# Two six-head tiles for the last twelve heads of a memory attention, with a regrouping of phi(q) through DRAM, and a two-part memset ahead of the first products

## The chip, the cores and the metric

One core of a Trainium2 chip runs the kernel. The metric is the device time of one execution in microseconds; the time before is the median of three runs. All views of the profile come from one further execution, whose own time and span stand in the table below.

## The reference, cut to what matters

Two attention layers run side by side over 2048 positions, 640 channels, 32 heads of 20 channels, in bf16. Layer A works in four segments of 512 positions and carries a memory from segment to segment; layer B is a causal attention with a window of 256.

```python
for s in range(4):                       # layer A, per head
    p = softmax(qs @ ks.T * scale + mask)          # inside the segment
    a_dot = p @ vs
    pq = phi(qs)                                   # t + 1 if t > 0 else exp(t)
    a_mem = (pq @ M) / (pq @ z + 1e-6)             # what earlier segments left
    o = g * a_mem + (1 - g) * a_dot
    M = M + phi(ks).T @ vs                         # 20 x 20 per head
    z = z + phi(ks).sum(0)
out_A = o @ wo ;  out_B = windowed_softmax_attention(x_B) @ wo_B
```

The change touches only `pq @ M`, `pq @ z` and the updates of `M` and `z`.

## The kernel before, in words

**Stages.** Work goes in eight chunks of 512 positions, A0 B0 A1 B1 A2 B2 A3 B3. While one chunk is scored, the projections of the next run between its products. Scores of a head group (four heads, on rows 0, 32, 64 and 96) go from TensorE into a ring of three PSUM tiles `sc` (line 631); ScalarE takes the exponential into a ring of 12 SBUF tiles `pt` (line 647); GpSimd cuts the mask's triangles out of `pt` (`affine_select`, line 682), VectorE does so for small ends (line 664); TensorE multiplies `pt` with `v` (line 696, in the last chunk line 717); VectorE transposes the result (line 748); reciprocal and normalisation follow on VectorE and GpSimd (lines 768 to 802). Output goes through a DRAM scratch, a transposing DMA (line 835) and the last projection.

**Heads on tiles.** 128 rows hold four heads with a stride of 32 rows, so 20 of every 32 rows are used by heads 0 to 19 in five such tiles (`KT` = 5, groups `g` = 0 to 4). The 12 spare rows of every 32 hold the channels of the last 12 heads (`NM` = 20, `GAP` = 48). For the softmax part these rows are regrouped through DRAM into tiles 5 to 7 of `qA`, `kA`, `qB`, `kB` (`regroup`, lines 400 and 408: four stores and four loads each). For the memory part they are not: the list `MEM` names twelve pairs (row tile `m`, group `g`). Groups 0 to 4 have one pair each; group 5 has two, group 6 three, group 7 two.

**Memory.** `phi_q` (line 482) puts phi(q) into `pq`, five tiles of 128x512, by lines 463, 467 and 471. `phi_k` stores phi(k) to DRAM and loads it back transposed as `pkT` (line 497). `dm_job` (line 511) runs at the start of the B chunk that follows an A chunk, for segments 0, 1 and 2. It forms phi(k)^T v for all twelve pairs in two PSUM banks of six (line 526, 84 columns for a pair, 168 where two pairs share `m`), adds each bank to `mz` on VectorE (line 536), and has GpSimd write the masked bf16 copy `blk` (in the trace `MZ`): line 542 for the sums `z`, line 545 for `M`. `mem(g)` (line 725) then multiplies the pairs of a group with `pq`, in one bank: 12 products of 128x512 for a segment, in segments 1, 2 and 3.

**Order.** The order of instructions is not left to a scheduler. `Flow` holds a model of each engine's time (`on_pe`, `on_dve`, `on_pool`, `on_dma`), and `body` emits the next piece of work whose modelled time has come. Engines run their own queues in that order, so an instruction that waits holds back everything behind it on its engine. `yield t` in a job means that nothing more of the job is emitted before model time `t`; `mark` and `known` carry such times. DMAs are issued by SyncE, one queue in order, aside from a few on ScalarE's.

**Start.** `consts_mz` clears `blk` on VectorE (line 322), then `mz`. `warm_up` (line 215) multiplies these zeros while the first input is under way. `consts_mem` (line 273) makes the head masks `bm` on GpSimd, `consts_e` (line 303) the table `ez`.

Of the kernel before, what the change touches and what calls it, by code (L numbers as in the profile page):

```python
# [13 lines left out]
P = 128  # L14
# [13 lines left out]
QPOOL = 750.0  # L28
GAP = 48
NM = 20  # L30
MEM = [(0, 0), (1, 1), (2, 2), (3, 3), (4, 4), (0, 5),
       (1, 5), (1, 6), (2, 6), (3, 6), (3, 7), (4, 7)]
NE = 5
NOT = 4
NSC = 3
# [14 lines left out]
def mm_ns(n):  # L50
    return max(27.0, n / 2.4 + 2.5)
# [133 lines left out]
class _K:  # L185
# [29 lines left out]
    def warm_up(self, z):  # L215

        f = self.f
        ps, bi = self.bank()
        f.pe = max(f.pe, 1900.0)
        while f.pe + 700.0 < max(self.done[(0, "x", 0)], self.done[("wk_A", 0)]):  # L220
            self.wide(ps, z[:, 0:P], z[:, 0:L], L, True, True)
            f.flush()
        self.close(bi, f.seen)
# [49 lines left out]
    def consts_mem(self):  # L273

        nc, cp = self.nc, self.cp
        sel = cp.tile([P, self.KT, 12], F32, name="sel")
        own = cp.tile([P, 4], F32, name="own")

        def select(t, pattern, base, mul):
            nc.gpsimd.affine_select(out=t, in_=t, pattern=pattern, compare_op=ALU.is_ge,
                                    fill=0.0, base=base, channel_multiplier=mul)
        nc.gpsimd.memset(own[:], 1.0)
        select(own[:], [[-HD, 4]], 0, 1)
        select(own[:], [[HD, 4]], DH - 1, -1)
        nc.gpsimd.memset(sel[:], 1.0)
        for j in range(4):

            t, base = sel[HD * j:HD * j + HD], 12 * j - DH  # L290
            select(t, [[0, self.KT], [0, 12]], -DH, 1)
            select(t, [[GAP, self.KT], [-DH, 12]], base, 1)
            select(t, [[-GAP, self.KT], [DH, 12]], DH - 1 - base, -1)
        self.bm = bm = cp.tile([P, len(MEM), 4], F32, name="bm")
        self.ez = cp.tile([P, len(MEM), 4], F32, name="ez")
        nc.gpsimd.tensor_copy(out=bm[:, 0:self.KT, :],
                              in_=own[:].unsqueeze(1).to_broadcast([P, self.KT, 4]))
        flat = bm[:].rearrange("p x j -> p (x j)")
        for m, x, h0, n in ((0, 5, 0, 4), (1, 6, 0, 8), (2, 8, 4, 4), (3, 9, 4, 8), (4, 11, 8, 4)):
            nc.gpsimd.tensor_copy(out=flat[:, 4 * x:4 * x + n], in_=sel[:, m, h0:h0 + n])  # L300
        self.eps = cp.tile([P, G], F32, name="eps")

    def consts_e(self):

        nc, e = self.nc, self.e32
        for x0, x1, g in ((0, self.KT, 0), (5, 7, 5), (7, 10, 6), (10, 12, 7)):
            n = x1 - x0
            h = e[:, 4 * g:4 * g + (4 * n if x0 == 0 else 4)]
            h = (h.rearrange("p (x j) -> p x j", j=4) if x0 == 0 else
                 h.unsqueeze(1).to_broadcast([P, n, 4]))  # L310
            nc.gpsimd.tensor_tensor(out=self.ez[:, x0:x1, :], in0=self.bm[:, x0:x1, :], in1=h,
                                    op=ALU.mult)
        for j in range(4):
            rows = slice(HD * j, HD * j + HD)
            nc.gpsimd.tensor_single_scalar(
                out=self.eps[rows, :], in_=e[rows, :].rearrange(
                    "p (g j) -> p g j", j=4)[:, :, j], scalar=EPS, op=ALU.mult)

    def consts_mz(self):
        nc, cp = self.nc, self.cp  # L320
        self.blk = self.big.tile([P, len(MEM), 4, HD], BF16, name="MZ4")
        nc.vector.memset(self.blk[:], 0.0)
        self.mz = cp.tile([P, len(MEM), 4, VS], F32, name="mz")
        nc.vector.memset(self.mz[:], 0.0)

    def consts_ends(self):
# [184 lines left out]
    def dm_job(self, seg, pkT, v):  # L511


        nc, f = self.nc, self.f
        yield self.known("pkT", seg)
        W = 4 * VS
        half = len(MEM) // 2
        for x0 in (0, half):
            yield "bank"
            dM, bi = self.bank()  # L520
            x = x0
            while x < x0 + half:
                m, g = MEM[x]
                k = 2 if x + 1 < x0 + half and MEM[x + 1] == (m, g + 1) else 1
                for kt in range(LT):
                    nc.tensor.matmul(dM[:, W * (x - x0):W * (x - x0 + k)],
                                     lhsT=pkT[:, kt, P * m:P * m + P],
                                     rhs=v[:, kt, W * g:W * (g + k)],
                                     start=(kt == 0), stop=(kt == LT - 1))
                f.on_pe("full", 4 * mm_ns(max(W * k, P)), 4 * W * k)  # L530
                x += k
                if x < x0 + half:
                    yield 0.0
            dv = dM[:, 0:half * W].rearrange("p (x j c) -> p x j c", x=half, j=4)
            mz = self.mz[:, x0:x0 + half]
            nc.vector.tensor_tensor(out=mz, in0=dv, in1=mz, op=ALU.add)
            self.close(bi, f.on_dve(620.0, f.seen))
            f.open = False
        t = f.dve + 138.0
        yield self.known(2 * seg, "avs")  # L540
        blk, mz = self.blk, self.mz
        nc.gpsimd.tensor_tensor(out=blk[:, :, :, DH], in0=mz[:, :, :, DH], in1=self.ez[:],
                                op=ALU.mult)
        f.on_pool(150.0, t)
        nc.gpsimd.tensor_tensor(out=blk[:, :, :, 0:DH], in0=mz[:, :, :, 0:DH],
                                in1=self.bm[:].unsqueeze(3)
                                .to_broadcast([P, len(MEM), 4, DH]), op=ALU.mult)
# [468 lines left out]
    def body(self, xA, A_wq, A_wk, A_wv, A_wo, A_beta, xB, B_wqkv, B_wo, out2d):  # L1016
# [59 lines left out]
        for nm, rows in (("pk", D), ("qA", 12 * DH), ("kA", 12 * DH), ("qB", 12 * DH),  # L1076
                         ("kB", 12 * DH)):
# [38 lines left out]
        while True:  # L1116
# [34 lines left out]
            if pend:  # L1151
                n, g, what = pend[0]
                kind, c = chunks[n]
                if what == "tile":
                    ps_ = [p for x in range(4) for p in parts[(n, g[1] + x)]
                           if p[1] // P == g[0]]
                    need = [whole(p[6] for p in ps_), self.done.get((n, "v", g[1]))]
                elif what == "av":
                    ps_ = parts[(n, g)]
                    need = [whole(p[6] for p in ps_), self.done.get((n, "v", g))]  # L1160
                else:
                    need = [self.done.get(("dm", c - 1))] + [self.done.get((n, "pq", m))
                                                            for m, g_ in MEM if g_ == g]
# [198 lines left out]
```

## Time and profile before

| | |
|---|---|
| median of 3 runs | 353.37 us (351.37, 353.37, 354.8) |
| the profiled execution | 352.71 us, span 350.6 us |
| first score in each chunk | A0 9.29, B0 55.48, A1 95.31, B1 132.68, A2 176.71, B2 213.39, A3 254.99, B3 291.74 us |
| GpSimd busy without idle time | 128.8 to 170.2 us |
| last exponentials on ScalarE | up to 332 us |

Columns of a group's line: the line and engine, the operation, output and inputs, shapes, how often; then busy time in us and the mean of one in ns; then the idle time of that engine just before, and who ended it. PE is TensorE's products, PEld its weight loads, DVE VectorE, ACT ScalarE, POOL GpSimd, SP SyncE, whose DMA issues count as waiting but not as busy.

Four groups that the change touches:

```profile
L735 PE MATMUL m<-pq,MZ 128*128 128x512 bf16 x36 | 11.9, 384 | 1.4 <-DVE vB L573 0.6 <-DVE tt L748 0.4 <-DVE kB L445 0.3
L526 PE MATMUL m<-vA,pkT 128*128 128x84 bf16 x96 | 5.5, 201 | 0.0
L536 DVE TENSOR_TENSOR mz<-m,mz 128x504 f32<-128x504 f32 x6 | 4.0, 662 | 1.0 <-PE m L526 1.0
L542 POOL TENSOR_TENSOR MZ<-mz,ez 128x48 bf16<-128x48 f32 x3 | 2.1, 695 | 1.2 <-DVE mz L536 1.2
```

Products overlap: 384 ns is from the start of one to the end of its results, while the next one in a row starts 0.22 us later.

### The profile page before, as it was taken

What the parts mean: (1) busy time and instruction counts of PE and PEld (TensorE: products, weight loads), DVE (VectorE), ACT (ScalarE), POOL (GpSimd) and SP (SyncE); (2) the same over time, 40 slices, a digit from 0 to 9 for tenths busy, and PEclk for the clock granted to TensorE, in tenths of its full rate; (3) what the DMA queues carried; (4) which work ended last, traced back from release to release, by engine and by line L of the source; (5) the groups of instructions that cost most, each with busy time, mean ns of one, the idle gap of its engine ahead of it and who ended that gap; (6) DMA issues with size and microseconds to landing.
All of it is one profiled execution on the core that took longest, in us unless ns stands there. A gap on an engine that the chain in (4) does not pass through costs nothing.

```text
span 350.6 us, 13578 instructions
## 1 busy us (share of the span) xinstructions
PE 326.4 (93%) x5617; PEld 167.0 (48%) x5617; DVE 278.2 (79%) x557; ACT 315.0 (90%) x358; POOL 294.3 (84%) x592
## 2 busy tenths in 40 slices
PE   7999999989999999999999999988999999899994
PEld 2443435444544345455644436454543445566672
DVE  5687677999958999999967998997867999766621
ACT  2897499999999999999999999999999999989831
POOL 6589388988898989999898989899988989987720
PEclk9999999999999999999999999999999999999999
DMA  7945617526675133033794025030483032675773
GB/s 233 376 159 129 165 32 227 128 64 178 200 124 123 22 77 122 2 93 69 175 193 104 0 63 155 3 79 8 82 143 77 2 75 61 146 140 150 146 183 115
DMA packets 69374, 40.54 MB, mean 116 GB/s; under 512 B 48448, under 2 KB 67520, under 8 KB 69312
## 3 DMA queue, kind: packets, MB, share of 16 engines
q1 hardware_dynamic: 67584, 38.35, 45.2%
q10 hardware_dynamic: 1728, 1.32, 1.2%
q8 instruction: 44, 0.72, 0.9%
q14 instruction: 18, 0.15, 0.1%
HBM read 16.06 MB, written 16.38 MB: 93 GB/s over the span
## 4 chain that ended last, share of the span: by engine, by line
PE 48%; DVE 22%; POOL 11%; issue 6%; ACT 5%; DMA 5%; SPq 2%; DVEq 0%; ACTq 0%; POOLq 0%
PE m L735 30%; PE sc L631 9%; POOL pt L682 7%; PE m L696 6%; ACT pt L647 5%; DVE tt L748 4%; DVE pt L664 3%; DMA xT<-in_B_x_dram 2%; PE m L717 2%; DMA scr_o<-o 2%; POOL o L782 2%; DVE kB L445 1%; PE sc L735 1%; DVE pq L471 1%; DVE qA L445 1%
## 5 line engine op out<-in xcount | busy, mean ns | idle before, releaser
L647 ACT ACTIVATE pt<-sc 128x1024 bf16<-128x1024 f32 (+1 forms) x320 | 296.6, 1070 | 14.9 <-PE sc L631 12.9
L682 POOL TENSOR_SCALAR_AFFINE_SELECT pt<-pt 128x256 bf16<-128x256 bf16 x448 | 209.6, 495 | 36.0 <-ACT pt L647 30.8
L748 DVE STREAM_TRANSPOSE tt<-m 128x512 f32<-128x512 f32 x88 | 60.7, 706 | 19.4 <-PE m L696 9.4
L782 POOL TENSOR_TENSOR o<-tt,rr 128x320 bf16<-128x320 f32 x64 | 51.2, 801 | 2.8 <-DVE rr L774 2.7
L631 PE MATMUL sc<-qB,kB 20*64 20x64 bf16 (+2 forms) x1728 | 39.0, 217 | 1.2 <-issue 0.6
L735 PEld LDWEIGHTS <-xT 128*128 128x128 bf16 x320 | 28.7, 97 | 22.4 <-issue 11.6
L735 PEld LDWEIGHTS <-oT 128*128 128x128 bf16 x320 | 28.8, 97 | 17.2 <-issue 3.5
L631 PE MATMUL sc<-qA,kA 20*128 20x128 bf16 (+3 forms) x512 | 36.1, 300 | 0.9 <-ACT pt L647 0.3
L631 PEld LDWEIGHTS <-kB 20*64 20x64 bf16 (+1 forms) x1728 | 21.7, 98 | 25.1 <-issue 23.1
L735 PE MATMUL m<-wv_A,xT 128*128 128x320 bf16 x160 | 27.4, 300 | 3.7 <-DVE kA L445 2.0
L891 DVE CAST ot<-m 128x320 bf16<-128x320 f32 x46 | 21.9, 480 | 8.5 <-PE m L735 8.3
L735 PE MATMUL m<-xT,wq_A 128*128 128x512 bf16 x100 | 26.6, 386 | 1.1 <-DVE qA L445 0.9
L664 DVE TENSOR_TENSOR pt<-pt,ends 128x1024 bf16<-128x1024 bf16 x32 | 27.6, 875 | 0.0
L735 PE MATMUL m<-xT,wk_A 128*128 128x512 bf16 x100 | 27.2, 392 | 0.3
L735 PE MATMUL m<-xT,wBq 128*128 128x512 bf16 x100 | 25.8, 380 | 1.2 <-DVE tt L748 1.2
L735 PE MATMUL m<-xT,wBk 128*128 128x512 bf16 x100 | 25.3, 381 | 0.6 <-DVE kB L445 0.6
L735 PE MATMUL m<-wBv,xT 128*128 128x320 bf16 x160 | 25.6, 300 | 0.3 <-DVE tt L748 0.2
L631 PEld LDWEIGHTS <-kA 20*128 20x128 bf16 x512 | 10.5, 91 | 30.5 <-issue 29.8
L696 PE MATMUL m<-pt,vA 128*32 128x128 bf16 (+3 forms) x512 | 24.0, 302 | 0.5 <-POOL pt L682 0.3
L735 PE MATMUL m<-wo_A,oT 128*128 128x320 bf16 x120 | 20.8, 300 | 0.2 <-DVE ot L891 0.2
L802 POOL TENSOR_TENSOR o<-o,u 128x320 bf16<-128x320 bf16 x24 | 20.5, 854 | 0.0
L445 DVE CAST qB<-m 128x512 bf16<-128x512 f32 x20 | 13.6, 682 | 7.4 <-PE m L735 7.4
(87 smaller groups left out, 427.7 us busy)
## 6 DMA issues: line engine op xcount, KB each, us to landing
scr_o<-o SPq DMA_DIRECT2D x28, 160.0 KB
out_dram<-ot SPq DMA_DIRECT2D x27, 160.0 KB
xT<-in_B_x_dram SPq DMA_DIRECT2D x4, 720.0 KB
scr_pk<-e SPq DMA_DIRECT2D x15, 128.0 KB
xT<-in_A_x_dram SPq DMA_DIRECT2D x3, 640.0 KB
scr_kA<-kA SPq DMA_DIRECT2D x16, 60.0 KB
scr_qA<-qA SPq DMA_DIRECT2D x16, 60.0 KB
kA<-scr_kA SPq DMA_DIRECT2D x16, 60.0 KB
```

The lines of the kernel that those rows point to most:

```text
L445: nc.vector.tensor_copy(out=dst[:, m, at:at + L], in_=ps[:, :])
L631: nc.tensor.matmul(ps[j // 2][h0:h1, j % 2, c0:c0 + nq], lhsT=k[rows, g, kc + h0:kc + h1], rhs=q[rows, g, q0:q0 + nq], start=True, stop=Tr ...
L647: nc.scalar.activation(out=pt[:, :, lo:hi], in_=ps[i][:, :, lo:hi], func=ACT.Exp, scale=self.scale)
L664: nc.vector.tensor_tensor(out=blk, in0=blk, in1=self.ends[:].unsqueeze(1).to_broadcast([P, 1024 // SH, SH]), op=ALU.mult)
L682: nc.gpsimd.affine_select(out=blk, in_=blk, pattern=pat, compare_op=ALU.is_ge, fill=self.zero, base=base, channel_multiplier=mul)
L696: nc.tensor.matmul(O[HD * j:HD * j + HD, q0:q0 + nq], lhsT=v[:, VS * h:VS * h + HD], rhs=pts[j // 2][:, j % 2, c0:c0 + nq], start=(n_ == 0 ...
L717: nc.tensor.matmul(O[HD * j:HD * j + HD, o0:o0 + nq], lhsT=v[:, VS * h:VS * h + HD], rhs=pts[j // 2][:, j % 2, c0:c0 + nq], start=(n_ == 0 ...
L735: self.nc.tensor.matmul(ps[:, 0:n], lhsT=lhsT, rhs=rhs, start=start, stop=stop)
L748: self.nc.vector.transpose(out=tt[:], in_=O[:, :])
L782: nc.gpsimd.tensor_tensor(out=dst, in0=a, in1=b, op=ALU.mult)
L802: nc.gpsimd.tensor_tensor(out=dst, in0=dst, in1=u[:], op=ALU.add)
L891: nc.vector.tensor_copy(out=ot[:, 320 * hf:320 * hf + 320], in_=ps[:, 0:320])
```

## The change

Groups 5 to 7 no longer take their phi(q) from the spare rows of five tiles. The 240 spare rows of `pq` are written to a DRAM scratch by four stores and loaded as a new tile `pq2`: two tiles of 120 rows, six heads each (heads 20 to 25 and 26 to 31). `MEM2` names four pairs: group 5 from the first tile, group 6 from both, group 7 from the second. A segment's memory product is thus 5 + 4 = 9 products, the last four with 120 rows.

The columns of `pkT` that belong to the spare rows are copied by GpSimd to a new tile `pkS`, so that 120 of them stand together as weights. `dm_job` has five products of 84 columns and two of 168 (each over four position tiles): one bank of 420 columns, one of 336 and 120 rows. `mz`, `blk`, `bm` and `ez` have nine pairs for twelve. The mask of the twelve heads is made by two selects for twelve.

`blk` is cleared in two parts, the first four pairs first, the warm-up reads only these, and its modelled start is 1500 ns for 1900.

```diff
-MEM = [(0, 0), (1, 1), (2, 2), (3, 3), (4, 4), (0, 5),
-       (1, 5), (1, 6), (2, 6), (3, 6), (3, 7), (4, 7)]
+MEM2 = [(1, 6), (0, 5), (1, 7), (0, 6)]
+R2 = 120
@@ warm_up
-        f.pe = max(f.pe, 1900.0)
+        f.pe = max(f.pe, 1500.0)
@@ consts_mem
-        sel = cp.tile([P, self.KT, 12], F32, name="sel")
...
-        for j in range(4):
-            t, base = sel[HD * j:HD * j + HD], 12 * j - DH
-            select(t, [[0, self.KT], [0, 12]], -DH, 1)
-            select(t, [[GAP, self.KT], [-DH, 12]], base, 1)
-            select(t, [[-GAP, self.KT], [DH, 12]], DH - 1 - base, -1)
...
+        sel = bm[:, self.KT:, :]
+        nc.gpsimd.memset(sel, 1.0)
+        select(sel, [[-2 * DH, 4], [-DH, 4]], 2 * DH, 1)
+        select(sel, [[2 * DH, 4], [DH, 4]], -DH - 1, -1)
@@ consts_e
-        for x0, x1, g in ((0, self.KT, 0), (5, 7, 5), (7, 10, 6), (10, 12, 7)):
+        for x0, x1, g in [(0, self.KT, 0)] + [(self.KT + x, self.KT + x + 1, g)
+                                              for x, (_, g) in enumerate(MEM2)]:
@@ consts_mz
-        nc.vector.memset(self.blk[:], 0.0)
+        nc.vector.memset(self.blk[:, 0:4], 0.0)
+        nc.vector.memset(self.blk[:, 4:], 0.0)
@@ phi_q
+        def store(t):
+            for j in range(4):
+                nc.sync.dma_start(
+                    out=scratch[:, :].rearrange("(m j r) s -> j r m s", m=self.KT, j=4)[j],
+                    in_=self.pq[HD * j + DH:HD * j + HD, :, :])
+                tl = f.on_dma(1, 280.0, t)
+            f.at(tl - 150.0, lambda: load(tl))
+        def load(t):
+            nc.sync.dma_start(out=self.pq2[0:R2], in_=scratch[:, :].rearrange(
+                "(h p) s -> p h s", p=R2))
+            self.mark(f.on_dma(1, 900.0, t), n, "pq2")
         def then(m, e, es, t):
             self.done_with(es, t)
             self.mark(t, n, "pq", m)
+            left[0] -= 1
+            if left[0] == 0:
+                f.at(t, lambda: store(t))
@@ dm_job
+        nc.gpsimd.tensor_copy(
+            out=spare[:].rearrange("p k (u r) -> p (k u) r", r=HD - DH),
+            in_=pkT[:].rearrange("p k (u c) -> p (k u) c", c=HD)[:, :, DH:])
+        there = f.on_pool(1000.0)
+        own = [(lambda kt, m=m: pkT[:, kt, P * m:P * m + P], P, [m], m) for m in range(KT)]
+        for some in (own, [(lambda kt, h=h: spare[:, kt, R2 * h:R2 * h + R2], R2,
+                            [x for x in range(4) if MEM2[x][0] == h], None) for h in (1, 0)]):
+            if some is not own:
+                yield there
             yield "bank"
...
-            self.close(bi, f.on_dve(620.0, f.seen))
+            self.close(bi, f.on_dve(100.0 + 1.04 * at, f.seen))
...
-        self.mark(f.on_pool(2200.0), "dm", seg)
+        self.mark(f.on_pool(1700.0), "dm", seg)
@@ mem
-        xs = [x for x in range(len(MEM)) if MEM[x][1] == g]
+        if g < self.KT:
+            self.wide(O, self.blk[:, g, :, :].rearrange("p j c -> p (j c)"), self.pq[:, g, :], L,
+                      True, True)
+            return O, bi
+        xs = [x for x in range(4) if MEM2[x][1] == g]
         for x in xs:
-            self.wide(O, self.blk[:, x, :, :].rearrange("p j c -> p (j c)"),
-                      self.pq[:, MEM[x][0], :], L, x == xs[0], x == xs[-1])
+            self.wide(O, self.blk[0:R2, self.KT + x, :, :].rearrange("p j c -> p (j c)"),
+                      self.pq2[0:R2, MEM2[x][0], :], L, x == xs[0], x == xs[-1])
@@ body
-        self.warm_up(self.blk[:].rearrange("p x j c -> p (x j c)"))
+        self.warm_up(self.blk[:, 0:4].rearrange("p x j c -> p (x j c)"))
```

The main loop waits for `(n, "pq2")` in place of the pairs' `pq` tiles before it emits `mem(g)` for groups 5 to 7.

More of the change, by code (lines that the diff above doesn't have):

```diff
@@ L277, in consts_mem @@
         nc, cp = self.nc, self.cp
-        sel = cp.tile([P, self.KT, 12], F32, name="sel")
-        own = cp.tile([P, 4], F32, name="own")
         def select(t, pattern, base, mul):
@@ L283, in select @@
                                     fill=0.0, base=base, channel_multiplier=mul)
+        own = cp.tile([P, 4], F32, name="own")
         nc.gpsimd.memset(own[:], 1.0)
@@ L286, in consts_mem @@
         select(own[:], [[HD, 4]], DH - 1, -1)
-        nc.gpsimd.memset(sel[:], 1.0)
-        for j in range(4):
-            t, base = sel[HD * j:HD * j + HD], 12 * j - DH
-            select(t, [[0, self.KT], [0, 12]], -DH, 1)
-            select(t, [[GAP, self.KT], [-DH, 12]], base, 1)
-            select(t, [[-GAP, self.KT], [DH, 12]], DH - 1 - base, -1)
-        self.bm = bm = cp.tile([P, len(MEM), 4], F32, name="bm")
-        self.ez = cp.tile([P, len(MEM), 4], F32, name="ez")
+        self.bm = bm = cp.tile([P, self.KT + 4, 4], F32, name="bm")
+        self.ez = cp.tile([P, self.KT + 4, 4], F32, name="ez")
         nc.gpsimd.tensor_copy(out=bm[:, 0:self.KT, :],
                               in_=own[:].unsqueeze(1).to_broadcast([P, self.KT, 4]))
-        flat = bm[:].rearrange("p x j -> p (x j)")
-        for m, x, h0, n in ((0, 5, 0, 4), (1, 6, 0, 8), (2, 8, 4, 4), (3, 9, 4, 8), (4, 11, 8, 4)):
-            nc.gpsimd.tensor_copy(out=flat[:, 4 * x:4 * x + n], in_=sel[:, m, h0:h0 + n])
+        sel = bm[:, self.KT:, :]
+        nc.gpsimd.memset(sel, 1.0)
+        select(sel, [[-2 * DH, 4], [-DH, 4]], 2 * DH, 1)
+        select(sel, [[2 * DH, 4], [DH, 4]], -DH - 1, -1)
         self.eps = cp.tile([P, G], F32, name="eps")
@@ L305, in consts_e @@
         nc, e = self.nc, self.e32
-        for x0, x1, g in ((0, self.KT, 0), (5, 7, 5), (7, 10, 6), (10, 12, 7)):
+        for x0, x1, g in [(0, self.KT, 0)] + [(self.KT + x, self.KT + x + 1, g)
+                                              for x, (_, g) in enumerate(MEM2)]:
             n = x1 - x0
-            h = e[:, 4 * g:4 * g + (4 * n if x0 == 0 else 4)]
-            h = (h.rearrange("p (x j) -> p x j", j=4) if x0 == 0 else
-                 h.unsqueeze(1).to_broadcast([P, n, 4]))
+            h = e[:, 4 * g:4 * g + 4 * n].rearrange("p (x j) -> p x j", j=4)
             nc.gpsimd.tensor_tensor(out=self.ez[:, x0:x1, :], in0=self.bm[:, x0:x1, :], in1=h,
@@ L320, in consts_mz @@
         nc, cp = self.nc, self.cp
-        self.blk = self.big.tile([P, len(MEM), 4, HD], BF16, name="MZ4")
-        nc.vector.memset(self.blk[:], 0.0)
-        self.mz = cp.tile([P, len(MEM), 4, VS], F32, name="mz")
+        self.blk = self.big.tile([P, self.KT + 4, 4, HD], BF16, name="MZ4")
+        nc.vector.memset(self.blk[:, 0:4], 0.0)
+        nc.vector.memset(self.blk[:, 4:], 0.0)
+        self.mz = cp.tile([P, self.KT + 4, 4, VS], F32, name="mz")
         nc.vector.memset(self.mz[:], 0.0)
@@ L482, in phi_q @@
     def phi_q(self, n):
+        nc, f = self.nc, self.f
+        left = [self.KT]
+        scratch = self.scr["pq"][n // 2]
+        def store(t):
[9 more added lines that the diff above has]
+            self.mark(f.on_dma(1, 900.0, t), n, "pq2")
         def then(m, e, es, t):
@@ L516, in dm_job @@
         W = 4 * VS
-        half = len(MEM) // 2
-        for x0 in (0, half):
+        KT = self.KT
+        spare = self.pkS
+        nc.gpsimd.tensor_copy(
[7 more added lines that the diff above has]
+                yield there
@@ L519, in dm_job @@
             yield "bank"
             dM, bi = self.bank()
[L521 to L524, printed above, removed]
+            at = 0
+            for lhs, rows, xs, g0 in some:
+                gs = [g0] if g0 is not None else sorted(MEM2[x][1] for x in xs)
+                n = W * len(gs)
                 for kt in range(LT):
-                    nc.tensor.matmul(dM[:, W * (x - x0):W * (x - x0 + k)],
-                                     lhsT=pkT[:, kt, P * m:P * m + P],
-                                     rhs=v[:, kt, W * g:W * (g + k)],
+                    nc.tensor.matmul(dM[0:rows, at:at + n], lhsT=lhs(kt),
+                                     rhs=v[:, kt, W * gs[0]:W * gs[0] + n],
@@ L529, in dm_job @@
                                      start=(kt == 0), stop=(kt == LT - 1))
-                f.on_pe("full", 4 * mm_ns(max(W * k, P)), 4 * W * k)
-                x += k
-                if x < x0 + half:
+                f.on_pe("full", 4 * mm_ns(n), 4 * n)
+                at += n
+                if (rows, xs) != (some[-1][1], some[-1][2]):
                     yield 0.0
-            dv = dM[:, 0:half * W].rearrange("p (x j c) -> p x j c", x=half, j=4)
-            mz = self.mz[:, x0:x0 + half]
+            rows = some[0][1]
@@ L536, in dm_job @@
+            dv = dM[0:rows, 0:at].rearrange("p (x j c) -> p x j c", j=4, c=VS)
+            if rows == P:
+                mz = self.mz[:, 0:KT]
+            else:
+                mz = self.mz[0:rows, KT:].rearrange("p (b a) j c -> p a b (j c)", a=2)
+                dv = dv.rearrange("p (a b) j c -> p a b (j c)", a=2)
             nc.vector.tensor_tensor(out=mz, in0=dv, in1=mz, op=ALU.add)
-            self.close(bi, f.on_dve(620.0, f.seen))
+            self.close(bi, f.on_dve(100.0 + 1.04 * at, f.seen))
@@ L546, in dm_job @@
                                 in1=self.bm[:].unsqueeze(3)
-                                .to_broadcast([P, len(MEM), 4, DH]), op=ALU.mult)
-        self.mark(f.on_pool(2200.0), "dm", seg)
+                                .to_broadcast([P, KT + 4, 4, DH]), op=ALU.mult)
+        self.mark(f.on_pool(1700.0), "dm", seg)
     def v_job(self, n, half, w_ap, v, gate, needs):
@@ L1051, in body @@
         self.pq = big.tile([P, KT, L], BF16, name="pq")
+        self.pq2 = big.tile([P, 2, L], BF16, name="pq2")
+        self.pkS = big.tile([P, LT, 12 * DH], BF16, name="pkS")
         self.qB = big.tile([P, G, L], BF16, name="qB")
@@ L1075, in body @@
         self.scr = scr = {}
-        for nm, rows in (("pk", D), ("qA", 12 * DH), ("kA", 12 * DH), ("qB", 12 * DH),
+        for nm, rows in (("pk", D), ("qA", 12 * DH), ("kA", 12 * DH), ("qB", 12 * DH), ("pq", 12 * DH),
                          ("kB", 12 * DH)):
@@ L1161, in body @@
                 else:
-                    need = [self.done.get(("dm", c - 1))] + [self.done.get((n, "pq", m))
-                                                            for m, g_ in MEM if g_ == g]
+                    need = [self.done.get(("dm", c - 1)),
+                            self.done.get((n, "pq", g) if g < KT else (n, "pq2"))]
                 if None not in need and not (f.open and 0 < f.left <= 3):
```

## The prediction

> **What bounds the kernel now.** I read the page first, for engine totals and chain, then the busy time by stage, then the waits of ScalarE and TensorE, and last GpSimd's timeline at the place where the change puts new work.
>
> The page's totals and its chain:
>
> ```profile
> PE 326.4 (93%) x5617; PEld 167.0 (48%) x5617; DVE 278.2 (79%) x557; ACT 315.0 (90%) x358; POOL 294.3 (84%) x592
> ...
> PE 48%; DVE 22%; POOL 11%; issue 6%; ACT 5%; DMA 5%; SPq 2%; DVEq 0%; ACTq 0%; POOLq 0%
> ```
>
> The chain blames TensorE (48%), and the change takes work from TensorE. But the chain names what ended last, and says nothing of the next engine in line. The stages do (columns: length, then busy us and count of PE, PEld, DVE, ACT, POOL; clock; DMA share; GB/s). They are B0, A1, B1, A2, B2, A3, B3 and the tail:
>
> ```profile
> 55.00:95.00 40.00, 36.92 (x805) 20.25 (x798) 37.24 (x69) 38.73 (x51) 35.63 (x69) 1.00 0.60 157
> 95.00:131.00 36.00, 34.51 (x409) 14.78 (x407) 30.03 (x68) 35.99 (x40) 32.73 (x63) 1.00 0.46 94
> 133.00:170.00 37.00, 34.26 (x746) 19.28 (x737) 35.03 (x67) 36.05 (x44) 37.00 (x67) 1.00 0.29 74
> 177.00:212.00 35.00, 34.02 (x430) 14.87 (x427) 28.82 (x65) 35.00 (x39) 32.07 (x62) 1.00 0.46 93
> 213.00:254.00 41.00, 37.75 (x907) 21.39 (x900) 35.69 (x68) 39.48 (x46) 38.43 (x75) 1.00 0.27 65
> 255.00:291.00 36.00, 34.97 (x433) 15.14 (x432) 29.55 (x67) 36.00 (x40) 32.12 (x61) 1.00 0.39 73
> 291.00:332.00 41.00, 38.45 (x1134) 24.56 (x1133) 29.25 (x63) 38.88 (x42) 35.15 (x76) 1.00 0.58 134
> 332.00:350.60 18.60, 13.47 (x156) 9.29 (x153) 4.75 (x9) 3.91 (x7) 2.95 (x7) 1.00 0.52 143
> ```
>
> ScalarE is full in the A stages (idle 0.01, 0.00, 0.00 us). In B0, B1 and B2 it idles 1.27, 0.95 and 1.52 us: 3.74 us is all that freed TensorE time can win there, and 2.12 us in B3. In B1 GpSimd has not one idle moment (37.00 of 37.00). So time is to be won at the head, in ScalarE's holes in the B stages, and nowhere else.
>
> The waits, as who waited for whom, total, times, longest:
>
> ```profile
> ACT pt L647 <- PE sc L631: 12.9, 18, 5.0
> ...
> PE m L696 <- POOL pt L682: 0.6, 2, 0.3
> ```
>
> ScalarE's holes end when a score arrives, so earlier TensorE work can fill some of them. TensorE hardly ever waits for a mask (0.6 us in all), though GpSimd runs late.
>
> **The change part by part.** *Memory products.* Their starts in a row are 0.22 us apart (133.07, 133.29, 133.51). Three fewer in a segment save 0.66 us: one in group 5, still in the A stage (126.39, 207.29, 285.63), worth nothing there, and two in groups 6 and 7 at the start of the next B stage, 0.44 us for each of B1, B2, B3.
>
> *phi(k)^T v.* In B0 a run of 24 products of 84 columns lasts 1.08 us, the last taking 0.20, so 0.038 us apart; those of 168 columns start 0.073 apart. Before, 32 and 8: 1.80 us. After, 20 and 8: 1.34. Saved 0.46 us in each of B0, B1, B2.
>
> So TensorE is relieved by 0.46 us in B0, 0.90 in B1 and B2, 0.44 in B3, 2.7 us in sum, all within some 6 us of a 40 us stage. Bounds of the gain: 0 and 2.7. The holes of the B stages (3.74 + 2.12 us) are spread over their whole length, so I take 6/40 of them, 0.9 us, less a third for what doesn't fit: -0.6 us.
>
> *GpSimd.* Rows of before (the first is the number of elements that the new copy has, the others the one-operand masks):
>
> ```profile
> L545 POOL TENSOR_TENSOR MZ<-mz,bm 128x960 bf16<-128x960 f32 x3 | 5.4, 1813 | 0.0
> L682 POOL TENSOR_SCALAR_AFFINE_SELECT pt<-pt 128x256 bf16<-128x256 bf16 x368 | 163.9, 472 | 27.4 <-ACT pt L647 23.1 <-PE m L735 1.8
> L682 POOL TENSOR_SCALAR_AFFINE_SELECT pt<-pt 128x512 bf16<-128x512 bf16 x64 | 42.0, 663 | 8.6 <-ACT pt L647 7.8
> ```
>
> No copy of 128x960 is in the trace. By busy time a mask costs 163.9/368 = 0.445 us for 256 elements and 42.0/64 = 0.656 for 512: 0.82 ns an element, so 960 elements 1.02 us. Lower end, the slope alone: 0.79. Upper end, a two-operand instruction of that size: 1.81. I take 1.02, since one operand is read, as by the masks. It gives back: line 545 goes from 960 to 720 elements. With 0.72 us for 320 elements (line 782 in the timeline) its slope is 1.71 ns, so -0.41; line 542 goes from 48 to 36, -0.15. Net +0.46 us per segment, from +0.2 to +1.3.
>
> [...]
>
> What does a later GpSimd cost? Its timeline in B1:
>
> ```profile
> 140.91 0.89 POOL L542 TENSOR_TENSOR MZ<-mz,ez 128x48 bf16<-128x48 f32 x1
> 141.65 1.81 POOL L545 TENSOR_TENSOR MZ<-mz,bm 128x960 bf16<-128x960 f32 x1
> 143.42 2.55 POOL L682 TENSOR_SCALAR_AFFINE_SELECT pt<-pt 128x256 bf16<-128x256 bf16 x6
> ```
>
> Pairing exponentials and masks in order, a mask starts 1.8 us after its exponential at 130 to 140 us, 4.9 us after at 145 to 150, 1 us at 165. These two instructions make that lag, and TensorE still waits for no mask longer than 0.3 us. So 0.46 us more lag is mostly cover used up: +0.15 us in each stage, +0.4 in sum. Where the cover is gone, net cost goes through one to one: up to +1.3 per stage, +3.9.
>
> *A new wait.* TensorE now waits for the copy `pkS` before its last eight phi(k)^T v products; behind it in TensorE's queue stand scores, and ScalarE has three `sc` tiles to live on, 0.9 us each. Copies queue behind masks: in B1 from about 132.7 + 1.8 to 135.5 us, while the 20 products ahead end near 135.2: +0.2 us, +1.0 if the copy takes 1.81. In B0 and B2 the lag at 55 and 214 us is 0.5 us: nothing. The copy itself waits for `pkT`, issued at 38.3, 97.0 and 180.2 us, long before 55.5, 132.7 and 213.4.
>
> *VectorE.* Two additions of 504 columns become 420 and 336: 252 columns less, at 1.0 ns (512 columns 0.68 us, 320 columns 0.48) 0.25 us per segment. I take 0, at most -0.25 each.
>
> *SyncE.* Five DMAs more in each of three segments: four stores at the 1.57 us that four `kA` stores take, one load of 0.4, and a wait for the stores of at most 2.7 (the longest for `scr_kB`): under 4.7 us. Behind it stand the regrouped `kA` (89.8 us; group 5 of A1 is scored after 111), the next `xT`, phi(k) and `pkT` (97 us, wanted at 133), and output stores. All have over 20 us. `pq2` is there some 7 us after the last `pq` (89.4, 169.6, 249.0), its first reader comes at 126.4, 207.3, 285.6: 36 us to spare. Cost 0; with the cover gone, 4.7 us a segment.
>
> *The head.* The memset of 768 words takes 698 ns, that of 1008 words 898: 0.83 ns a word, so 256 words take 0.27 us and the first zero product starts at 1.36 for 1.79. Products of 512 columns start 0.427 us apart up to 7.41, and 0.216 apart from 7.69. If full pace keeps its 5.75 us from the first product, it comes 0.43 us sooner: -0.2 us. Products at 4.15, 4.75 and 5.32 stand further apart than 0.427, so they waited for input; only the five from 5.70 to 7.41 can be halved: -1.1 at most, 0 at least. I take -0.3; TensorE is busy 9.88 and 9.37 us of the next two 10 us, so it carries on. [...] Fewer mask instructions at the start cost and gain nothing (GpSimd idles from 6.95 to 10.82 us), nor does one more in `consts_e` (busy 6.30 of the 10 us from 40 to 50).
>
> Sum: -0.6 + 0.4 + 0.2 - 0.3 = -0.3 us. On the profiled 352.7 us (span 350.6 and 2.1 around it) this gives 352.4; the median is 0.7 above that execution, so 353.1.
>
> **The rivals.** *Slower: GpSimd is the bound in B1 and B2.* For: no idle moment from 128.8 to 170.2 us, and masks of 256 elements start 0.37 us apart at best but many 0.8, so the copy may take 1.81. Price: 1.3 per stage plus 1.0 of TensorE's wait in B1 and half that in B2, +5.4: 358.5. It decides once more than 1.2 us per stage reaches ScalarE. Against: 0.6 us of waits for masks. *Faster: TensorE is what ends the holes.* All 2.7 us arrive, and 1.1 from the head: 349.6. For: every hole ends with a score. Against: TensorE is 92% busy in B0 to B2, ScalarE 96 to 97%, so little is left to fill. *It doesn't do what it says:* the early zeros may bring no earlier clock (the warm-up only becomes longer), and the order may shift through the changed bookings in `Flow`; both stay inside the spread of the three times, 3.4 us.
>
> **How the numbers follow.** Within 1% (349.8 to 356.9), about what a measurement of this kernel can tell from no change: 0.65, the forecast and the last rival. Slower 0.18, faster 0.17. The forecast's own range is 350.5 to 355.5. Two in ten left out, the range reaches halfway into both rivals: 349.8 to 357.3.
>
> **What would show it.** `m<-pq,MZ` at 27 products and line 526's successor at 84; a copy near 1.0 us on GpSimd; ScalarE still full in the A stages; ScalarE's idle time in B0 to B2 between 3 and 4.5 us; mask lag in B1 peaking near 5.4 us; first zero product near 1.36. Wrong would be: TensorE waiting for `pkS` over 1 us, a wait for `pq2` ahead of group 5, or a pace change at 4 us and all stages 1 us sooner.

## The result, and the profile after

The changed kernel is slower, by about one per cent.

| | before | after |
|---|---|---|
| median of 20 runs each | 352.25 us (350.38 to 354.8) | 355.71 us (352.64 to 360.33) |
| ratio, 95% interval | | 1.0098 (1.0074 to 1.0122) |
| profiled execution, span | 352.71 us, 350.6 us | 355.05 us, 353.0 us |
| first exponential, last exponential | 9.7, 332.0 us | 8.9, 336.7 us |
| ScalarE idle from the 41st exponential to the last | 6.1 us | 10.7 us |
| from the last exponential to the end | 18.6 us | 16.3 us |

The last three rows are read from ScalarE's timeline. The 41st exponential is the first after the long hole of chunk A0.

The page's totals and chain of after:

```profile
PE 322.0 (91%) x5535; PEld 165.6 (47%) x5573; DVE 277.8 (79%) x561; ACT 314.2 (89%) x357; POOL 292.3 (83%) x581
...
PE 26%; POOL 22%; DVE 18%; ACT 13%; DMA 10%; issue 7%; SPq 2%; ACTq 0%; DVEq 0%; POOLq 0%
```

TensorE has 4.4 us less to do, GpSimd 2.0, ScalarE 0.8, and the span is 2.4 us longer. No engine's work grew; they wait more, and the chain is now spread over all of them. Busy time by stage, columns as before, for B0, A1, B1, A2, B2, A3, B3 and the tail:

```profile
56.00:97.00 41.00, 37.70 (x794) 20.46 (x792) 38.19 (x73) 39.24 (x52) 36.79 (x73) 1.00 0.68 165
97.00:133.00 36.00, 34.32 (x410) 15.53 (x418) 29.86 (x67) 36.00 (x40) 32.08 (x61) 1.00 0.49 102
133.50:179.60 46.10, 41.27 (x904) 23.23 (x901) 41.86 (x82) 42.76 (x52) 43.57 (x79) 0.96 0.47 115
179.60:217.30 37.70, 35.49 (x447) 15.77 (x452) 30.85 (x68) 36.91 (x41) 33.08 (x62) 1.00 0.31 66
217.30:258.80 41.50, 38.25 (x888) 22.14 (x888) 36.28 (x69) 39.66 (x46) 40.72 (x79) 1.00 0.40 87
258.80:295.70 36.90, 35.40 (x444) 15.59 (x447) 30.35 (x68) 36.76 (x41) 32.82 (x62) 1.00 0.29 65
295.70:336.70 41.00, 37.84 (x1126) 24.24 (x1119) 28.99 (x63) 38.19 (x41) 35.15 (x77) 1.00 0.57 134
336.70:353.00 16.30, 10.50 (x133) 6.94 (x130) 3.54 (x7) 3.19 (x5) 2.21 (x4) 0.99 0.50 140
```

ScalarE idles 1.76, 3.34 and 1.84 us in B0, B1 and B2 (length less its busy time; 1.27, 1.15 and 1.52 in before, whole chunks too), and A2 is no longer full (0.79). The waits, as who waited for whom, total, times, longest:

```profile
ACT pt L676 <- PE sc L660: 16.5, 18, 5.0
...
PE m L725 <- POOL pt L711: 2.6, 3, 1.8
```

ScalarE's waits for scores grew from 12.9 to 16.5 us, TensorE's for masks from 0.6 to 2.6. Two holes of ScalarE can be followed through the timeline (start, busy us, instruction, count; in brackets the idle time ahead of it and who ended it):

```profile
160.47 0.29 PE L725 MATMUL m<-pt,vX 128*32 128x256 bf16 x4 [1.76 <-POOL pt L711]
...
162.91 1.94 ACT L676 ACTIVATE pt<-sc 128x1024 bf16<-128x1024 f32 x2 [1.03 <-PE sc L660]
...
176.03 1.84 SPq L939 DMA_DIRECT2D out_dram<-ot  x2
...
181.72 0.49 DVE L924 CAST ot<-m 128x320 bf16<-128x320 f32 x1 [1.67 <-DMA out_dram<-ot]
182.26 0.38 PE L768 MATMUL m<-xT,wBk 128*128 128x512 bf16 x1 [0.73 <-DVE ot L924]
183.09 3.77 ACT L676 ACTIVATE pt<-sc 128x1024 bf16<-128x1024 f32 x4 [0.80 <-PE sc L660]
```

In the first, a `pt v` product stands in TensorE's queue ahead of scores and waits 1.76 us for a GpSimd mask; ScalarE runs dry 1.03 us. In the second, VectorE's cast waits for an output store to free its tile, TensorE for the cast, ScalarE for TensorE. ScalarE has eleven holes above 0.3 us after A0, for six before; the longest, 1.55 us at 334.74, ends with a GpSimd mask. No one place holds the loss: after's 61st exponential comes 1.4 us later than before's, the 181st 3.8, the 221st 5.3, the last one 4.65, of which the tail gives back 2.3.

Behind the first hole the granted clock of TensorE fell to half for 3.41 us (columns as above, the clock third from the end):

```profile
158.09:161.50 3.41, 1.64 (x96) 1.03 (x84) 2.91 (x5) 3.41 (x6) 3.41 (x7) 1.00 1.12 282
161.50:164.91 3.41, 3.08 (x82) 1.49 (x71) 2.08 (x6) 2.32 (x3) 3.41 (x8) 0.50 0.44 67
```

In the 3.41 us before the fall TensorE had been busy for only 1.64. What such stretches cost can be estimated from the 245 runs on record that have a clock and enter a ratio: among runs of one kernel, 0.01 less clock went with 1.5 us more, give or take 0.5. After's runs averaged 0.992 and those of before 0.998, so some 0.9 of the 3.5 us goes with the clock, and most does not.

The new work itself, by groups and timeline:

```profile
L533 POOL COPY pkS<-pkT 128x960 bf16<-128x960 bf16 x3 | 3.0, 1014 | 0.0
L574 POOL TENSOR_TENSOR MZ<-mz,bm 128x720 bf16<-128x720 f32 x3 | 4.2, 1401 | 0.0
L768 PE MATMUL m<-pq,MZ 128*128 128x512 bf16 x15 | 5.7, 382 | 1.2 <-DVE vB L602 0.6
L768 PE MATMUL m<-pq,MZ 120*128 120x512 bf16 x12 | 4.1, 386 | 0.2 <-DVE ot L924 0.2
L550 PE MATMUL m<-vA,pkT 128*128 128x84 bf16 x60 | 2.8, 200 | 0.0
L550 PE MATMUL m<-vA,pkS 128*120 128x168 bf16 x24 | 2.3, 237 | 0.3 <-DVE mz L565 0.2
```

All of it has the forecast's counts, and durations close to the forecast's. That poses the question: why is a kernel slower whose pieces cost what they were to cost?

### The profile page after: what moved, and what is told of

Same layout as the page of the kernel before. It is cut to its first block, busy times and chain, and to the rows that moved or that the text cites. A ratio compares the mean times of both kernels' runs of the same rounds, so it can differ in the third digit from the quotient of the medians.

```text
span 353.0 us, 13474 instructions
## 1 busy us (share of the span) xinstructions
PE 322.0 (91%) x5535; PEld 165.6 (47%) x5573; DVE 277.8 (79%) x561; ACT 314.2 (89%) x357; POOL 292.3 (83%) x581
## 3 DMA queue, kind: packets, MB, share of 16 engines
q10 hardware_dynamic: 1584, 1.16, 1.1%
## 4 chain that ended last, share of the span: by engine, by line
PE 26%; POOL 22%; DVE 18%; ACT 13%; DMA 10%; issue 7%; SPq 2%; ACTq 0%; DVEq 0%; POOLq 0%
PE m L768 16%; POOL pt L711 14%; ACT pt L676 13%; PE sc L660 5%; DVE tt L781 3%; POOL o L815 3%; PE m L725 3%; POOL o L835 3%; DMA scr_qA<-qA 2%; DMA wv_A<-in_A_wv_dram 2%; DMA out_dram<-ot 2%; DVE pt L693 2%; DMA scr_o<-o 1%; DVE vA L597 1%; DVE qA L439 1%
## 5 line engine op out<-in xcount | busy, mean ns | idle before, releaser
L676 ACT ACTIVATE pt<-sc 128x1024 bf16<-128x1024 f32 (+1 forms) x320 | 296.9, 1076 | 20.1 <-PE sc L660 16.5
L924 DVE CAST ot<-m 128x320 bf16<-128x320 f32 x50 | 24.3, 485 | 9.6 <-PE m L768 7.6
L768 PE MATMUL m<-xT,wq_A 128*128 128x512 bf16 x89 | 24.4, 380 | 2.8 <-DMA wq_A<-in_A_wq_dram 0.9
L693 DVE TENSOR_TENSOR pt<-pt,ends 128x1024 bf16<-128x1024 bf16 x32 | 26.5, 834 | 0.0
L768 PE MATMUL m<-xT,wBk 128*128 128x512 bf16 x89 | 24.4, 381 | 1.6 <-DVE ot L924 0.7
L768 PE MATMUL m<-wo_A,oT 128*128 128x320 bf16 x130 | 22.3, 300 | 0.4 <-DVE ot L924 0.3
L768 PE MATMUL m<-wo_B,oT 128*128 128x320 bf16 x120 | 20.3, 300 | 1.8 <-issue 1.5
```

The source lines that it names most:

```text
L676: nc.scalar.activation(out=pt[:, :, lo:hi], in_=ps[i][:, :, lo:hi], func=ACT.Exp, scale=self.scale)
L693: nc.vector.tensor_tensor(out=blk, in0=blk, in1=self.ends[:].unsqueeze(1).to_broadcast([P, 1024 // SH, SH]), op=ALU.mult)
L768: self.nc.tensor.matmul(ps[:, 0:n], lhsT=lhsT, rhs=rhs, start=start, stop=stop)
L924: nc.vector.tensor_copy(out=ot[:, 320 * hf:320 * hf + 320], in_=ps[:, 0:320])
```

## The experiments

Theories. **Work**: something among the new instructions costs more than its duration (the five DMAs in SyncE's queue, the copy ahead of masks, the wait for `pkS`). **Order**: the change books other durations in `Flow` (TensorE's 4 products, VectorE's 620 ns, GpSimd's 1000 and 1700 for 2200, a wait `there`), so that the loop emits other instructions at other places; the work is harmless, the order is not. The copy and the head are taken apart further down. Every ratio is to the kernel before in the same series (medians 352.68, 352.73, 352.11 and 351.97 us; 352.25 for after). The kernel before with the copy alone, planned too, has no time on record.

| kernel | work | order | median us | ratio (95%) | ScalarE idle us |
|---|---|---|---|---|---|
| before | old | old | | 1 | 6.1 |
| after | new | new | 355.71 | 1.0098 (1.0074 to 1.0122) | 10.7 |
| DMAs alone | old + 5 DMAs | old | 352.31 | 0.9975 (0.995 to 1.0001) | 6.8 |
| new work, old order | new | old | 351.09 | 0.9962 (0.994 to 0.9984) | 6.2 |
| old work, new order | old | new | 356.12 | 1.0113 (1.008 to 1.0146) | 9.9 |
| TensorE and VectorE bookings | old | another | 357.06 | 1.0138 (1.0092 to 1.0185) | 9.1 |
| GpSimd bookings | old | another | 353.7 | 1.0024 (0.9996 to 1.0052) | 9.0 |
| one booking + 10% | old | another | 358.26 | 1.0172 (1.0126 to 1.0218) | 9.8 |
| one booking - 2.5% | old | another | 352.69 | 1.0013 (0.9981 to 1.0044) | 6.1 |
| after, same booking + 10% | new | another | 355.29 | 1.0078 (1.0041 to 1.0114) | 9.2 |
| after, GpSimd booked as measured | new | another | 357.51 | 1.0149 (1.0097 to 1.0201) | 8.9 |
| before, GpSimd booked as measured | old | another | 354.07 | 1.0066 (1.0037 to 1.0095) | 8.6 |
| new work, old order, early copy | new | old | 350.43 | 0.9949 (0.9923 to 0.9974) | 4.1 |
| the same, second copy | new + 3 copies | old | 351.99 | 0.9989 (0.9957 to 1.0021) | 4.8 |
| two-part memset alone | old, new head | old | 351.65 | 0.999 (0.9965 to 1.0015) | 6.6 |

### Is it the DMAs?

The kernel before, with the four stores and the load of the change, not booked in `Flow`; nothing reads `pq2`.

```diff
...
+        def store(t):
+            for j in range(4):
+                nc.sync.dma_start(
+                    out=scratch[:, :].rearrange("(m j r) s -> j r m s", m=self.KT, j=4)[j],
+                    in_=self.pq[HD * j + DH:HD * j + HD, :, :])
+            f.at(t + 3700.0, load)
...
+        def load():
+            nc.sync.dma_start(out=self.pq2[0:120], in_=scratch[:, :].rearrange(
+                "(h p) s -> p h s", p=120))
...
```

> The kernel before, with the four stores of phi(q)'s spare rows and the load of them added on SyncE in each of three segments, not booked, all else in its old place. Nobody reads the loaded tile. Theory WORK in its SyncE form (output stores behind them come late, VectorE waits for an output buffer): +0.5 to +1.5 us, with a wait of VectorE for an output store between 170 and 190 us. Theory ORDER: within 0.3 us of before.

Ratio 0.9975 (0.995 to 1.0001). The order is that of before but for the DMAs. VectorE's wait for an output store near 180 us is absent. The DMAs cost nothing that shows: the forecast's 0 holds.

### Work or order?

Two crossed kernels. The first has all of the change's work and books it at the old durations, as if it were the old work (`k` follows the old pairs, and the copy and the DMAs are booked at nothing):

```diff
...
-                f.on_pe("full", 4 * mm_ns(n), 4 * n)
...
+                f.on_pe("full", 4 * mm_ns(max(W * k, P)), 4 * W * k)
...
-            self.close(bi, f.on_dve(100.0 + 1.04 * at, f.seen))
+            self.close(bi, f.on_dve(620.0, f.seen))
...
-        self.mark(f.on_pool(1700.0), "dm", seg)
+        self.mark(f.on_pool(2200.0), "dm", seg)
```

> All work of the change (nine products, the copy, the DMAs, the two-part memset), but booked in the planner at the old costs, so that what is common to both kernels is issued in the order of before. Theory WORK: +2 to +3.5 us against before, as the change. Theory ORDER: -1 to 0 us.

The second has all of the old work and books it at the change's durations, with its hold-back `there`, its modelled DMAs and its start:

```diff
...
+        there = f.on_pool(1000.0)
...
-                f.on_pe("full", 4 * mm_ns(max(W * k, P)), 4 * W * k)
...
+                n = W * (1 + part)
+                f.on_pe("full", 4 * mm_ns(n), 4 * n)
...
-            self.close(bi, f.on_dve(620.0, f.seen))
+            self.close(bi, f.on_dve(100.0 + 1.04 * (336 if part else 420), f.seen))
...
-        self.mark(f.on_pool(2200.0), "dm", seg)
+        self.mark(f.on_pool(1700.0), "dm", seg)
```

> The mirror: all work of before (twelve products, no copy, no extra DMAs, memset in one part), booked at the costs of the change, so that what is common is issued in the order of the change. Theory WORK: within 1 us of before. Theory ORDER: +2.5 to +4.5 us.

New work in the old order: 0.9962, faster by 1.3 us. Old work in the new order: 1.0113, slower by 4.0 us. Together +2.7, beside +3.5 for the change, which the intervals allow. ScalarE's waits for scores in the first kernel (its ScalarE order is that of before, instruction for instruction), then the same row and TensorE's waits for masks of the second, whose ScalarE order is that of after:

```profile
ACT pt L673 <- PE sc L657: 13.4, 17, 5.0
```

```profile
ACT pt L666 <- PE sc L650: 17.0, 20, 5.0
...
PE m L715 <- POOL pt L701: 2.5, 3, 1.6
```

The second row of the second kernel is the one that after showed as new (2.6): it comes with no copy, no `pq2` and no shorter mask, with the order alone. The second kernel even has after's two waits at their places:

```profile
161.66 0.40 PE L715 MATMUL m<-pt,vX 128*32 128x256 bf16 x4 [1.59 <-POOL pt L701]
...
181.73 0.49 DVE L915 CAST ot<-m 128x320 bf16<-128x320 f32 x1 [0.81 <-DMA out_dram<-ot]
```

Its granted clock fell to half at 161.7 us, as after's did at 161.5 (the mean over 133 to 170 us is 0.95 in both), and averaged the same 0.992 over its runs. So the loss belongs to the order, its part that goes with the clock included, and the work gains.

### Which booking?

The old work with a part of the new bookings: those of TensorE and VectorE, or those of GpSimd.

```diff
...
-                f.on_pe("full", 4 * mm_ns(max(W * k, P)), 4 * W * k)
...
+                n = W * (1 + part)
+                f.on_pe("full", 4 * mm_ns(n), 4 * n)
...
-            self.close(bi, f.on_dve(620.0, f.seen))
+            self.close(bi, f.on_dve(100.0 + 1.04 * (336 if part else 420), f.seen))
```

> All work of before; only TensorE's and VectorE's bookings of the memory work are those of the change (28 products for 40, nine for twelve, the shorter additions). Theory SPECIFIC (one of the new bookings, the wait for the copy, makes the bad order): within 1 us of before. Theory LOTTERY (before's order is a good one that any disturbance of the planner loses): +1 to +4 us.

```diff
+        there = f.on_pool(1000.0)
         for x0 in (0, half):
+            if x0:
+                yield there
...
-        self.mark(f.on_pool(2200.0), "dm", seg)
+        self.mark(f.on_pool(1700.0), "dm", seg)
```

> All work of before; only GpSimd's bookings are those of the change: 1000 ns for a copy that isn't made, with the second bank held back until then, and 1700 for 2200 ns at the end. Theory SPECIFIC: +2.5 to +4 us, as the change. Theory LOTTERY: +1 to +4 us too, so this run alone doesn't tell.

1.0138 and 1.0024: +4.9 us, more than its expectation went to, and +0.8, less than either theory had. GpSimd's bookings alone do little that can be told, TensorE's and VectorE's as much as all together. Is it then what these bookings say, or that anything is changed? The old work with one booking 10% up, and 2.5% down, which stand for nothing in the kernel:

```diff
-                f.on_pe("full", 4 * mm_ns(max(W * k, P)), 4 * W * k)
+                f.on_pe("full", 4.4 * mm_ns(max(W * k, P)), 4 * W * k)
```

> All work of before; the booking of one phi(k)^T v product is 10% longer, a change with no meaning, which moves some 2000 of 11200 instructions of TensorE to other places. Theory SPECIFIC: within 1 us. Theory LOTTERY: +1 to +4 us.

```diff
-                f.on_pe("full", 4 * mm_ns(max(W * k, P)), 4 * W * k)
+                f.on_pe("full", 3.9 * mm_ns(max(W * k, P)), 4 * W * k)
```

> All work of before; the booking of one phi(k)^T v product 2.5% shorter, which moves 300 of TensorE's 11200 instructions. Theory LOTTERY (the old order is one of the best, any other loses): +0.5 to +3 us. If orders scatter evenly about before: anything from -2 to +2 us.

Counted on the traces where TensorE's instructions (weight loads among them) stand in another order than in before, the booking raised by 10% moves 1073 of 11,234 (the expectation's 2000 counted each in both lists), as many as the change's own bookings (1071), and gives 1.0172, more than the change. Its runs averaged a granted clock of 0.998, that of before. Lowered by 2.5% the booking moves 177 and costs nothing that can be told. GpSimd's bookings move 698 (+0.2%), TensorE's and VectorE's 1443 (+1.4%), the truer GpSimd bookings of the next part 1089 (+0.7%). So the loss goes with how much was moved, roughly and not in step. ScalarE's waits for scores in the kernel with TensorE's and VectorE's bookings, and in the one with 10% more:

```profile
ACT pt L649 <- PE sc L633: 15.7, 19, 5.0
```

```profile
ACT pt L647 <- PE sc L631: 18.1, 19, 5.0
```

The same booking 10% up in the changed kernel:

```diff
-                f.on_pe("full", 4 * mm_ns(n), 4 * n)
+                f.on_pe("full", 4.4 * mm_ns(n), 4 * n)
```

> The changed kernel, its work untouched, with the booking of one phi(k)^T v product 10% longer, which moves some 1100 of TensorE's 11100 instructions. Theory LOTTERY: the time differs from the changed kernel's by over 1 us, up or down (350 to 359 us). Theory SPECIFIC (the change's order is bad for a reason that this leaves in place): within 1 us of it.

1.0078 beside after's 1.0098: the intervals overlap. The expectation of a difference above 1 us for a random reshuffle fell; a reshuffle of an already poor order did not show as one.

### Are late masks what the new order costs?

GpSimd's masks take longer than `Flow` books (0.45 and 0.66 us measured, 0.37 and 0.59 booked). If TensorE's new waits for masks were the cause, truer bookings would cure it.

```diff
-QPOOL = 750.0
+QPOOL = 800.0
...
-            ready[x] = f.on_pool(150.0 + 0.86 * r, te)
+            ready[x] = f.on_pool(215.0 + 0.9 * r, te)
...
-                t3 = f.on_pool(717.0, t)
+                t3 = f.on_pool(850.0, t)
```

> The changed kernel with GpSimd booked at what the traces show: a mask of 256 elements 445 ns for 370, of 512 elements 676 for 590, the normalisation 800 for 750, the addition 850 for 717. The planner then issues products later where they wait for masks. Theory MASKS (the new order is bad since TensorE is sent to wait for masks that are late): TensorE's waits for GpSimd fall from 2.1 us to under 1, ScalarE's idle time from 10.7 to under 8.5, the time to 351 to 353.5. Theory LOTTERY (any order but the old one loses some, whatever the bookings): 353 to 358, ScalarE's idle time 8.5 to 11.

> The kernel before with the same four bookings. Theory MASKS: 350.5 to 352.5, no worse than before. Theory LOTTERY: +0.5 to +5 us.

1.0149 and 1.0066: truer bookings made the kernel before slower, and cured nothing in the changed one (1.0149 beside 1.0098, overlapping intervals). There TensorE's waits for masks fell to 0.4 us, yet ScalarE's waits for scores and one of its holes read:

```profile
ACT pt L676 <- PE sc L660: 18.2, 21, 5.3
...
237.29 1.94 ACT L676 ACTIVATE pt<-sc 128x1024 bf16<-128x1024 f32 x2 [3.39 <-PE sc L660]
```

A hole of 3.39 us at a place where after had none of that size: between two batches of scores TensorE's queue holds 18 projection products (2.97 us from 231.85) and a `pt v` product that waits 1.16 us for VectorE. So late masks are one form that the loss takes, not all of its cause: with few of them it came back elsewhere.

### The copy

In the crossed kernel (new work, old order) the copy is booked at nothing and issued where `dm_job` begins, so it does come late; here it is issued once `pkT` has landed, in the A stage.

```diff
+            f.at(self.done[("pkT", c)] + 1500.0, copy)
...
+        def copy():
+            nc.gpsimd.tensor_copy(
+                out=self.pkS[:].rearrange("p k (u r) -> p (k u) r", r=HD - DH),
+                in_=pkT[:].rearrange("p k (u c) -> p (k u) c", c=HD)[:, :, DH:])
@@ dm_job
-        nc.gpsimd.tensor_copy(
-            out=spare[:].rearrange("p k (u r) -> p (k u) r", r=HD - DH),
-            in_=pkT[:].rearrange("p k (u c) -> p (k u) c", c=HD)[:, :, DH:])
```

> All work of the change in the order of before, as e3, but GpSimd's copy is issued once the transposed phi(k) has landed, which for segments 1 and 2 is in the A stage, where GpSimd idles, in place of the B stage's start. In e3 TensorE waited 1.65 us for the copy at 135 us and ScalarE idled 2.4 us from 137 to 142. Theory WORK in what is left of it (the copy's wait costs e3 its place in B1): 1 to 2 us below e3. If ScalarE's holes there have another cause: as e3, within 0.5 us.

Ratio 0.9949, the lowest of all, yet only 0.5 us below the 0.9962 without the move, with overlapping intervals: the expected gain of 1 to 2 us is not shown. The first product that reads `pkS` in B1, ahead of the move and then with it:

```profile
135.23 0.57 PE L548 MATMUL m<-vA,pkS 128*120 128x168 bf16 x4 [1.65 <-DVE rr L800]
```

```profile
107.03 0.98 POOL L515 COPY pkS<-pkT 128x960 bf16<-128x960 bf16 x1
...
135.45 0.47 PE L551 MATMUL m<-vA,pkS 128*120 128x168 bf16 x4
```

The 1.65 us wait (the row names VectorE, which had long been done; it ends with the copy) is gone, and so are the ScalarE holes of 0.92, 0.61 and 0.86 us at 136.5 to 142 us. With the late copy the wait was followed by half clock, from 135.5 to 142.3 us, where those holes lie (the mean over 133 to 170 us is 0.91); with the early copy the clock stayed full there (1.00). Which of the two made the holes is not separated. To price GpSimd's time at that place, the same kernel with one more copy of that size at the start of B0, B1 and B2, to a tile that nothing reads:

```diff
+        nc.gpsimd.tensor_copy(
+            out=self.pkX[:].rearrange("p k (u r) -> p (k u) r", r=HD - DH),
+            in_=pkT[:].rearrange("p k (u c) -> p (k u) c", c=HD)[:, :, DH:])
...
```

> As e8 (the change's work, old order, early copy), with one more GpSimd copy of 960 elements into a tile that nobody reads, at the start of each of B0, B1 and B2. It prices GpSimd time in the B stages by itself. The prediction's term was +0.15 us per stage for 0.46 us: here 1.0 us per stage, so +0.3 to +1.0 us against e8 in all. Rival (GpSimd is the bound there, it goes through one to one): +2.5 to +3.5 us.

351.99 us, 0.9989: 0.40% above the early copy's ratio, 1.4 us for 3.0 us of GpSimd, 0.47 us for one. The two intervals overlap (0 to 2.9 us), so this is a size, not a proof. The expectation had 0.3 to 1.0 us, its rival 2.5 to 3.5. TensorE's waits for masks, with the early copy alone and with both:

```profile
PE m L725 <- POOL pt L711: 1.7, 3, 1.1
```

```profile
PE m L728 <- POOL pt L714: 4.2, 5, 1.1
```

### The head

The kernel before with the two-part memset, the short warm-up and the start at 1500 ns:

```diff
-        f.pe = max(f.pe, 1900.0)
+        f.pe = max(f.pe, 1500.0)
...
-        nc.vector.memset(self.blk[:], 0.0)
+        nc.vector.memset(self.blk[:, 0:4], 0.0)
+        nc.vector.memset(self.blk[:, 4:], 0.0)
...
```

> The kernel before with the memset of blk in two parts, the warm-up on the first part and its start at 1500 ns; all else is issued in the old order. The prediction's head term: first exponential 0.2 to 1.1 us earlier and the whole kernel -0.3 us. Rival: the first exponential comes earlier, but the weights' DMAs and the regrouping that A0 waits for near 41 us take it back: 0.0 us in the end.

0.999 (0.9965 to 1.0015). TensorE's first products of real input in that kernel:

```profile
4.31 2.31 PE L736 MATMUL m<-xT,wk_A 128*128 128x512 bf16 x5 [0.31 <-DMA wk_A<-in_A_wk_dram]
6.45 1.24 PE L736 MATMUL m<-xT,wq_A 128*128 128x512 bf16 x5
8.97 1.25 PE L736 MATMUL m<-xT,wk_A 128*128 128x512 bf16 x5 [1.28 <-DMA wk_A<-in_A_wk_dram]
```

Five products take 2.31 us at 4.31 and 1.24 us at 6.45: the pace doubles there, 1.24 us ahead of before's 7.69. Then TensorE waits 1.28 us for the weights `wk_A`, whose products start at 8.97 us, in before at 8.12: in this execution the gain went into waiting for a DMA. In after, with the same head, those products started at 7.29 and the first exponential came 0.8 us sooner than before's, but the 41st 0.7 us later.

## Why the prediction was wrong, point by point

**The step that failed** is the last rival's: "the order may shift through the changed bookings in `Flow`; [both] stay inside the spread of the three times, 3.4 us". The shift of order was named, priced by the spread of repeated runs, which says nothing of another order, and left out of the sum. It is the largest term: +4.0 us (+2.8 to +5.1) by the old work in the new order, beside a forecast sum of -0.3. The forecast of 353.1 lacked just this; its range, up to 357.3, held the time.

**The work was sized rightly in its parts, and a little low in its worth.** Forecast for work and head together -0.3 us; measured -1.3 (-2.1 to -0.6) with the late copy. Counts are as forecast (27 memory products, 84 of phi(k)^T v). The copy took 1.014 us (0.98 to 1.08) for the 1.02 worked out, line 545's successor 1.401 (0.41 less, as said); line 542's successor gave back 0.05 for 0.15. VectorE's additions save 0.24 us a segment. `pq2` is loaded at 94, 175 and 261 us and first read at 127, 211 and 290: no wait.

**The wait for `pkS`** was taken at 0.2 us: 0.12 us at 137.16 in after, but 1.65 in the old order, and issuing the copy earlier removed it. The wait of over 1 us, named as a sign of error, appears only there. Mask lag in B1 did not grow as foretold (to 5.4 us): masks and exponentials paired in order, the longest from the end of an exponential is 5.3 us in after, and was 5.4 in before.

**GpSimd's price** was forecast at 0.15 us for 0.46 (0.33 for one), by the slower rival at one for one; 0.47 was measured, with an interval that holds both 0.33 and nearly 1. The rival's end (slower) came true, its mechanism did not: in the old order the same GpSimd work leaves the kernel faster than before.

**The head** was taken at -0.3. Measured -0.4 us (-1.2 to +0.5), so nothing can be told. The first zero product came at 1.26 us for the 1.36 foretold. The pace change came sooner than in before's execution, but kernels with the memset in one part had it as early (6.01 us), so the memset is not shown to have moved it. The forecast's own sentence that three products "waited for input" was a warning that a faster pace may end in a wait for data.

**ScalarE's idle time** in B0 to B2 was to be 3 to 4.5 us and is 6.9 (before 3.9 by whole chunks; the prediction's B1 left out 170 to 177 us), with A2 no longer full: the row that shows the failed step in after itself. It could not tell order from work; the crossed kernels did.

**What stays open.** Why the old order is better than six of the eight others that were run (of GpSimd's bookings and the booking lowered by 2.5% it can't be told). Had it been picked among many by its measured time, the others would be expected to lie behind it, as they do (+0.1 to +1.7%); but that is argued, not shown. Nor is the loss one wait: in after it is masks, an output store and a stretch at half clock, in the kernel with truer bookings the largest hole is projection products ahead of scores. The clock's share is an estimate, and no run isolates it.

## What to carry to other kernels

Where a cost model emits the order, editing a booked duration is an edit of the whole program: price it apart from the work, by one kernel with the new work at the old bookings and one with the old work at the new. Keep an order that is known to run well (book the new work at the old costs) until a better one has been found by running it; truer bookings gave none here. This change in the old order, with the copy moved into the A stage, ran in 350.43 us, 0.9949 (0.9923 to 0.9974) of the kernel before, and beats both; the move's own share is not shown.

## What the runs showed of the hardware

A one-operand GpSimd copy of 960 bf16 elements a partition, in runs of twelve, took 0.98 to 1.08 us in after, and in the mean 0.98 us in the kernel with the early copy and 0.99 and 1.02 us in the one with a second copy: 1.02 to 1.13 ns an element with its fixed share. A mask instruction grew by 0.82 ns an element from 256 to 512 elements (0.445 and 0.656 us of busy time each in before).

The mean granted clock was 0.989 to 0.995 in nine of the fifteen profiled executions, and 0.999 to 1 in the other six. In after (0.995) it fell to half once before the tail, for 3.41 us from 161.50; in the 3.41 us ahead of the fall TensorE was busy for 48%. In after and in both crossed kernels a single wait of TensorE had come just before the half clock: 1.76 us up to 160.47 in after, 1.65 us up to 135.23 in the new work in the old order, 1.59 us up to 161.66 in the old work in the new order. In after, five products of 512 columns took 2.08 us at half clock (163.23) and 1.24 at full clock (7.29).

In after and in the kernel with the two-part memset alone, products stood 0.216 us apart from 6.00 and from 6.45 us on, 4.7 and 5.2 us after the first zero product (1.26 and 1.25); in the eight kernels with one part that began between 6.01 and 7.82 us (7.69 in before), all with the first zero product at 1.79. The second spread is wide, 1.8 us for one and the same start, and no run here isolates what makes it. Whatever sets it, the first score came at 8.47 us in after, at 10.16 with the two-part memset alone and at 9.29 in before.
